# Moving the in-weight forms of the attention part from GpSimd to VectorE

## The chip, the cores and the metric

The kernel runs on one core of a Trainium2 chip. A core has five engines that work side by side, each through its own instructions in order: TensorE (PE: matrix products, its weight loads are shown apart as PEld), VectorE (DVE), ScalarE (ACT), GpSimd (POOL) and SyncE (SP), which here only issues DMAs. The metric is the time of one execution on the device in microseconds (us). The kernel before the change takes 964.0 us, the median of 3 runs (963.87 to 964.06).

## The reference

An attention block with routing, and behind it a two-layer block with a gate. Cut to what matters:

```python
# q, k, v: (4, 8, 768, 64); centroids: (8, 16, 64)
q_assign = argmax(einsum('bhsd,hcd->bhsc', q_n, c_n))     # q_n, k_n, c_n: normed to length 1
k_assign = argmax(einsum('bhsd,hcd->bhsc', k_n, c_n))
mask = q_assign[:, :, :, None] == k_assign[:, :, None, :]
scores = where(mask, q @ k.T / sqrt(64), -1e9)
attn = exp(scores - max(scores)); attn = attn / (sum(attn) + 1e-9)
x = (attn @ v), as (3072, 512)                            # (batch, token) rows, (head, d) columns
h = x @ w_in                                              # w_in: (512, 2048)
g = h * erf(max(h, 0) + log1p(exp(-abs(h))))
out = g @ w_out                                           # w_out: (2048, 512)
```

## The kernel before

**Two parts.** The attention part comes first and takes the first 411 us or so. It goes through 16 *pairs* (a batch and two heads that lie in the two halves of the 128 partitions). The second part computes `x @ w_in` and `g @ w_out` in 2x2 blocks with seven block products in place of eight (in places in two levels, with fewer still). For this it needs sums and differences of blocks of the weights and of `x`. These sums and differences are called *forms*.

**The forms.** `left_forms` (line 632) lists four of them for one slice of `w_in`, `right_forms` (641) four for a slice of `x`. Each is one instruction that reads two tiles of 128 x 512 float32 in SBUF and writes one. Forms of a slice depend on each other: the first feeds the second, the third overwrites a block of `w_in` in place, the fourth needs the second. The kernel makes a list of forms before the attention part starts (1338 to 1340): four slices of `w_in`, so 16 forms, each entry with a version for VectorE (`[0]`) and one for GpSimd (`[1]`). Behind pair 13 four forms of the first chunk of `x` join the list (line 1513). Whoever makes the next form takes the first entry off the list, so the order of the forms is fixed and only the engine and the place differ.

**The periods.** `period(p, i)` (line 1344) writes the instructions of one sixth of a pair. There are two halves of the queries to a pair and six blocks of 128 keys to a half, hence 12 units; a period has two, `u` and `u + 1`, and three periods make a half. A period holds, in this order in each engine's own queue:

- *Maxima of the next pair* (`maxima_step`, 462). For the shift of the softmax the kernel needs row maxima ahead of time. TensorE multiplies low-precision copies into `wide`, a single PSUM buffer, and VectorE reduces it into `nmx` (0.96 us). A period has two such steps. Because `wide` is one buffer, TensorE refills it only after VectorE has reduced it.
- *Scores* (`products`, 513, and `scores`, 526). TensorE writes the products of queries and keys and the masks into `sc`, of which there are two buffers; ACT takes the exponential (`curve`, 540) into one of eight `pr` tiles.
- *Sums* (`accumulate`, 549). POOL adds the `pr` tiles of the period before into an accumulator, ten additions of 128 x 768 to a pair, 1.7 to 1.8 us each.
- *Products with v* (`attend`, 561), on TensorE into `turned`.
- *Division* (`divide`, 574), in periods 0 and 3, for the half that just ended. TensorE multiplies the accumulator with `minus` (the row sums), so it waits for POOL's last addition. ACT makes the inverse, VectorE multiplies (`den`, `turned`, `more_out`), and SP stores the result in four DMAs.
- *Routing of the pair after next* (`similarities`, 393, and `choose`, 406). In period 3 TensorE writes similarities, and VectorE transposes them (`sims`), takes their maxima and marks the winners (`hot`). These maxima lie in the score bank `sc` of the period's second unit, so TensorE can't reuse that bank before `hot` is made. The masks `km` and `qm` come of this in later periods; the one that VectorE makes in period 0 (`km`, 436) serves the prediction as a mark for a pair's start.
- *Weights*. The weights lie in memory as 64-bit numbers and are made into float32 in steps: up to pair 14, each pair converts two pieces, with ACT (`size`, `rest`, `sign`), VectorE (`bounded` and `shifted`, 0.4 us each: both in period 0, and one and one in period 3) and POOL (`summed`, 1.29 us, in periods 1 and 4, which also has SP fetch a further piece).
- *Forms*, as below.

The order within an engine is the order in which the program writes its instructions (`InOrder`, line 129); no planner moves them. Between the engines only semaphores order the work.

**Where the forms stand.** `FORMS` (line 41) says how many forms VectorE makes in which period of which pair: `FORMS[p][i]`. `POOL_FORMS` (line 42) says in which pairs POOL makes one. The lines are

```python
        for _ in range(min(len(forms), FORMS.get(p, {}).get(i, 0))):
            forms.pop(0)[0]()
        ...
            for w in (u - 2, u - 1):
                accumulate(w)
            if i == 4 and p in POOL_FORMS and forms:
                forms.pop(0)[1]()
```

VectorE's forms come after `bounded` and, in period 0, `shifted`; in period 3 they come between `bounded` and `sims`. POOL's come behind its additions of the period, and ahead of the next period's. What is left on the list behind the last pair is made by VectorE (line 1514), ahead of the last additions. Before the change VectorE makes 1 form each in the pairs 12 and 13 (period 0), 2 in pair 14 (periods 0 and 3), 7 in pair 15 and 1 behind the loop; POOL makes one each in the pairs 8 to 15, in period 4.

Of the kernel before, what the change touches and what calls it, by code (L numbers as in the profile page):

```python
# [28 lines left out]
HJ = NJ // 2  # L29
# [8 lines left out]
LC = 512  # L38

UP = 2.0**16  # L40
FORMS = {12: {0: 1}, 13: {0: 1}, 14: {0: 1, 3: 1}, 15: {0: 1, 3: 2, 4: 2, 5: 2}}
POOL_FORMS = range(8, 16)
BIG = 2.0**60
FLOOR = 2.0**50
EPS = 2.0**-70
# [100 lines left out]
def kernel(  # L146
# [174 lines left out]
    def bounded(n):  # L321
        w = w_steps[n][0]
        ve.tensor_scalar(out=w, in0=w, scalar1=2.0, scalar2=None, op0=ALU.max)
# [5 lines left out]
    def shifted(n):  # L329
        w = w_steps[n][0].bitcast(U32)  # L330
        ve.tensor_scalar(out=w, in0=w, scalar1=3, scalar2=None, op0=ALU.logical_shift_left)
# [61 lines left out]
    def similarities(p):  # L393

        if p >= NPAIR:
            return
        st = pairs[p]
        st["psim"] = turned[1][:, 0:HW]
        for g in range(4):
            te.matmul(  # L400
                st["psim"][2 * C * g : 2 * C * (g + 1)], lhsT=ccT[:, p % HP],
                rhs=st["qk"[g // 2] + "T"][:, (g % 2) * HW : (g % 2 + 1) * HW],
                start=True, stop=True,
            )
# [27 lines left out]
    def vectors(p, nm):  # L432
        if p < NPAIR:
            ae.copy(out=pairs[p][nm + "v"], in_=pairs[p][nm + "T"])

    def masks(p, nm, half, bank, narrow=False, copied_by=ae):

        if p >= NPAIR:
            return lambda: None
        st = pairs[p]  # L440
        cols = slice(half * HW, (half + 1) * HW)
        r, hot = slice(0, D) if nm == "q" else slice(D, P), st["hotT"]
        picked = pick[r, half]
        if narrow:
            r = slice(r.start + Q, r.stop)
            picked = pick[r, 1]
            hot = hot if half else st["aside"]
        won = bank[:, 0:HW]
        te.matmul(won, lhsT=picked, rhs=hot[r], start=True, stop=True)
        if nm == "q":  # L450
            return lambda: ae.activation(out=st["qm"][:, cols], in_=won, func=ACT.Relu)
        if copied_by is ve:
            return lambda: ve.tensor_scalar(
                out=st["km"][:, cols], in0=won, scalar1=BIG, scalar2=nbig, op0=ALU.mult, op1=ALU.add
            )
        return lambda: ae.activation(
            out=st["km"][:, cols], in_=won, func=ACT.Identity, bias=nbig, scale=BIG
        )
# [34 lines left out]
    def turn(p, h, copies=(ae.copy, ae.copy)):  # L493

        st = pairs[p]
        pn = turned[h][:, 0:HW].rearrange("p (t n) -> p t n", t=HJ)
        for t in range(HJ):
            for e in range(2):
                cols = slice(e * D, e * D + Q)
                te.matmul(pn[cols, t], lhsT=lowest[h][:, t, cols], rhs=identb, start=True, stop=True)  # L500
        for e, copy in zip(range(2), copies):
            r = slice(e * D, e * D + 1)
            copy(out=st["qm"][r, h * HW : (h + 1) * HW], in_=pn[r].rearrange("p t n -> p (t n)"))
        st["shift", h] = True
# [8 lines left out]
    def products(u):  # L513
        p, half, j = units[u]
        if u in sc_of:
            return
        st = pairs[p]
        sc = sc_of[u] = ps_s.tile([P, 2, 512], F32, name="sc", tag="s")
        for e in range(2):
            r = slice(e * D, (e + 1) * D)  # L520
            te.matmul(
                sc[:, e, 0:HW], lhsT=st["kT"][r, j * P : (j + 1) * P],
                rhs=st["qT"][r, half * HW : (half + 1) * HW], start=True, stop=False,
            )

    def scores(u, rows=Q):

        p, half, j = units[u]
        st = pairs[p]
        sc = sc_of[u]  # L530
        assert ("shift", half) in st
        for e in range(2):
            r = slice(e * D, (e + 1) * D)
            r = slice(r.start, r.start + rows)
            te.matmul(
                sc[:, e, 0:HW], lhsT=st["km"][r, j * P : (j + 1) * P],
                rhs=st["qm"][r, half * HW : (half + 1) * HW], start=False, stop=True,
            )

    def curve(u):  # L540

        pr = prs[u % NPT]
        sc = sc_of.pop(u)[:, :, 0:HW].rearrange("p e (c x) -> p e c x", c=2)
        ae.activation(out=pr[:, :, :, 0:QW], in_=sc, func=ACT.Exp, scale=D**-0.5)
# [780 lines left out]
    def run(work):  # L1325
        for _ in work:
            pass
# [3 lines left out]
    def step_ahead(u, behind=False):  # L1331
        p, i = divmod(u + NJ, 2 * NJ)
        steps = maxima_step(p, i, behind=behind) if p < NPAIR else iter(())
        if not behind:
            run(steps)
        return steps

    forms = []
# [5 lines left out]
    def period(p, i):  # L1344
        u = 2 * NJ * p + 2 * i
        n1, n2 = 2 * p - 1, 2 * p
        early = lambda n: 0 <= n < N_EARLY

        def mask(place):
            which = (MASKS if p else FIRST_MASKS).get((i, place))  # L1350
            if which:
                return masks(p + 1, *which, turned[0 if i in (0, 5) else 1], place > 1, ve if i == 0 else ae)
            return lambda: None

        if u > 0:
            for which in turns if i in (0, 3) else ():
                turn(*which)
                turns.remove(which)
            step_ahead(u)
        mask(0)()  # L1360
        next(part[0], None)
        if i == 5:
            next(routing[0], None)
        if i == 0 and p:
            run(routing[0])
        if u == 2:
            next(routing[0])
        products(u)
        products(u + 1)
        mask(1)()  # L1370
        second = step_ahead(u + 1, True) if u > 0 else iter(())
        next(second, None)
        rows = D if u == 0 or u + NJ >= len(units) else Q
        scores(u, rows)
        next(second, None)
        if i:
            next(second, None)
        next(part[0], None)
        scores(u + 1, rows)
        later = mask(2)  # L1380
        if i == 0:
            later()
            later = lambda: None
            next(second, None)
        if i == 3:
            similarities(p + 2)
            routing[0] = choose(p + 2, sc_of[u + 1][:, 0], True)
        curve(u)
        later()
        curve(u + 1)  # L1390
        if u == 0:
            step_ahead(1)
            similarities(1)
            routing[0] = choose(1, turned[0])
            next(routing[0])
            next(routing[0])
            vectors(1, "q")
            vectors(1, "k")
        if i == 0 and early(n1 - 1):
            bounded(n1 - 1)  # L1400
            shifted(n1 - 1)
            sign(n1 - 1)
        elif i == 1 and early(n1):
            size_and_rest(n1)
        elif i == 3 and early(n1):
            bounded(n1)
            sign(n1)
        elif i == 5 and early(n2):
            rest(n2)
        for _ in range(min(len(forms), FORMS.get(p, {}).get(i, 0))):  # L1410
            forms.pop(0)[0]()
        if i == 3:
            next(routing[0], None)
            if early(n1):
                shifted(n1)
            for _ in range(2):
                next(routing[0], None)
        elif i == 1:
            load(p + 1, "v", v, vp)
            if p == 0:  # L1420
                run(routing[0])
                transposes(2, "q")
        elif i == 2:
            transposes(p + 2, "k")
        elif i == 4:
            vectors(p + 2, "k")
            vectors(p + 2, "q")
        elif i == 5:
            transposes(p + 3, "q")
        if u > 0:  # L1430
            if i == 1 and early(n1 - 1):
                summed(n1 - 1)
            elif i == 4 and early(n1):
                summed(n1)
            for w in (u - 2, u - 1):
                accumulate(w)
            if i == 4 and p in POOL_FORMS and forms:
                forms.pop(0)[1]()
            for w in (u - 2, u - 1):
                attend(w)  # L1440
            if i % HJ == 0:
                part[0] = divide(u - 1)
                next(part[0])
        if i == 3 and early(n2):
            size(n2)
# [204 lines left out]
```

## Time and profile before

| | |
|---|---|
| time, median of 3 runs | 964.0 us |
| the profiled execution | 963.7 us |
| its span in the trace | 962.0 us |
| pairs 7 and 8, from `km` to `km` | 24.44, 24.43 us |
| pairs 9 to 13 | 24.97, 24.81, 24.79, 25.03, 25.04 us |
| end of the attention part on TensorE | 411.5 us |
| VectorE's form of 128 x 512 | 0.68 to 0.69 us in pairs 12 to 14; 0.80 to 2.18 us in pair 15 |
| POOL's form of 128 x 512 | 1.27 to 1.29 us |
| TensorE clock granted | 1.00 in the windows of the attention part |

The trace is read as follows. The page gives busy times of the engines and the chain of work that ended last. The order in time gives each instruction's start and duration, its engine and operation, the tiles it writes and reads (`nmx<-wide`), shapes, the number merged into one line, and in brackets how long the engine was idle before it and what ended that wait. Most lines of the kernel are recorded under one line, L137, the helper that passes instructions on; so instructions are told apart by their tiles. A form is a `TENSOR_TENSOR` of 128x512 whose tiles are `w_in`, `more_in`, `x_own` or `x_more`. The tile `more_out` is used for several things in the attention part, POOL's accumulators among them. A window gives the busy time of each engine between two moments.

### The profile page before, as it was taken

How to read it: one execution, taken by the hardware profiler on the slowest of the kernel's cores; microseconds unless marked ns; L12 is line 12 of the kernel's file. 1: busy time of each engine (PE TensorE's matmuls, PEld its weight loads, DVE VectorE, ACT ScalarE, POOL GpSimd, SP SyncE). 2: the span in 40 equal slices, each digit the busy share in tenths (PEclk: the TensorE clock that was granted, in tenths of full speed). 3: DMA queues.
4: the chain of work that ended last, by engine and by line, in shares of the span. 5: the costliest groups of instructions: out<-in, count | busy, mean ns of one | idle time of the engine just before them, and what ended most of it. 6: DMA issues, size and time to landing. Idle time of an engine off the chain costs nothing.

```text
span 962.0 us, 22444 instructions
## 1 busy us (share of the span) xinstructions
PE 951.8 (99%) x8954; PEld 727.4 (76%) x8954; DVE 798.2 (83%) x1399; ACT 538.9 (56%) x815; POOL 531.4 (55%) x371
## 2 busy tenths in 40 slices
PE   8999999999999999999999999999999999999998
PEld 3555555555555555588888888998999899989987
DVE  8888888888888887787579889788868987897887
ACT  3777777777777777552523541654257236625541
POOL 1688888888888888887479910360054016202600
PEclk9999999999999999999999999999999999999999
DMA  9354444454453521051404444363445336343433
GB/s 220 65 111 112 111 111 111 112 112 110 106 111 76 126 57 54 23 174 44 165 1 163 164 136 141 133 204 112 155 123 174 112 129 209 110 147 119 159 114 110
DMA packets 172313, 116.06 MB, mean 121 GB/s; under 512 B 131376, under 2 KB 141104, under 8 KB 172208
## 3 DMA queue, kind: packets, MB, share of 16 engines
q1 hardware_dynamic: 169280, 113.41, 42.1%
q8 instruction: 71, 1.16, 0.5%
q10 hardware_dynamic: 2928, 1.21, 0.4%
q14 instruction: 34, 0.28, 0.1%
HBM read 90.21 MB, written 24.38 MB: 119 GB/s over the span
## 4 chain that ended last, share of the span: by engine, by line
PE 96%; DVE 2%; DMA 1%; POOL 0%; issue 0%; ACT 0%; SPq 0%; DVEq 0%; POOLq 0%
PE bank L137 42%; PE turned L137 31%; PE sc L137 17%; PE wide L137 6%; DVE nmx L137 1%; DVE km L137 0%; POOL more_out L137 0%; DMA in_k<-in_k_dram 0%; SPq L137 0%; DMA in_q<-in_q_dram 0%; DVE kT L137 0%; ACT qm L137 0%; DVE sims L137 0%; DVE qT L137 0%; ACT pr L137 0%
## 5 line engine op out<-in xcount | busy, mean ns | idle before, releaser
L137 POOL TENSOR_TENSOR more_out<-more_out,pr 128x768 f32<-128x768 f32 x128 | 217.1, 1696 | 15.7 <-ACT pr L137 6.8
L137 DVE TENSOR_REDUCE nmx<-wide 128x2 f32<-128x768 f32 x189 | 180.5, 955 | 47.1 <-PE wide L137 46.5
L137 ACT ACTIVATE pr<-sc 128x768 f32<-128x768 f32 x192 | 148.8, 810 | 89.7 <-PE wide L137 76.0
L137 POOL TENSOR_TENSOR g<-g 128x512 f32<-128x512 f32 x36 | 47.1, 1309 | 217.2 <-DVE g L137 215.3
L137 PE MATMUL turned<-pr,in_v 128*32 128x193 f32 x3072 | 144.9, 330 | 0.0
L137 PEld LDWEIGHTS turned<-pr,in_v 128*32 128x32 f32 x3072 | 91.5, 109 | 50.7 <-issue 21.3
L137 PE MATMUL sc<-qT,kT 64*128 64x384 f32 x528 | 98.4, 486 | 0.0
L137 DVE TENSOR_TENSOR g<-g 128x512 f32<-128x512 f32 x114 | 79.1, 694 | 16.5 <-PE bank L137 12.9
L137 DVE TENSOR_TENSOR g<-bank,g 128x256 f32<-128x256 f32 (+1 forms) x129 | 63.9, 523 | 16.2 <-PE bank L137 9.1
L137 DVE TENSOR_TENSOR g<-a_s,g 128x512 f32<-128x512 f32 x80 | 72.4, 932 | 5.6 <-ACT a_s L137 5.6
L137 PE MATMUL bank<-w_out,g 128*128 128x256 f32 x328 | 75.7, 380 | 0.0
L137 ACT ACTIVATE a_s<-g 128x1024 f32<-128x1024 f32 (+1 forms) x36 | 41.0, 1149 | 56.3 <-POOL g L137 45.7
L137 PE MATMUL bank<-g_more,g 128*128 128x256 f32 x304 | 71.8, 379 | 0.0
L137 PE MATMUL bank<-x_own,w_in 128*128 128x128 f32 (+1 forms) x432 | 71.6, 308 | 0.0
L137 POOL TENSOR_TENSOR more_out<-pr,pr 128x768 f32<-128x768 f32 x32 | 59.3, 1853 | 19.9 <-ACT pr L137 19.9
L137 PEld LDWEIGHTS bank<-w_out,g 128*128 128x128 f32 x328 | 62.0, 190 | 9.6 <-issue 1.4
L137 PEld LDWEIGHTS <-qv 64*128 64x128 bf16 x384 | 26.9, 93 | 53.4 <-issue 37.3
L137 PEld LDWEIGHTS sc<-qT,kT 64*128 64x128 f32 x528 | 50.1, 187 | 21.3 <-ACT inv L137 3.1
L137 PE MATMUL wide<-kv,qv 64*128 64x384 bf16 x378 | 64.3, 328 | 1.2 <-ACT km L137 0.6
L137 ACT ACT_TABLE_LOAD x40 | 51.3, 1283 | 23.0 <-DVE g L137 22.4
L137 PEld LDWEIGHTS bank<-x_own,w_in 128*128 128x128 f32 x432 | 61.1, 191 | 4.0 <-issue 0.6
L137 PEld LDWEIGHTS bank<-g_more,g 128*128 128x128 f32 x304 | 57.8, 190 | 7.9
(244 smaller groups left out, 2059.5 us busy)
## 6 DMA issues: line engine op xcount, KB each, us to landing
g_more<-b_dram SPq DMA_DIRECT2D x48, 512.0 KB, 3.5
g_more<-w_dram SPq DMA_DIRECT2D x84, 256.0 KB, 2.8
x_own<-in_moe_w_in_dram SPq DMA_DIRECT2D x13, 512.0 KB, 5.1
in_v<-in_v_dram SPq DMA_DIRECT2D x32, 192.0 KB, 3.1
x_dram<-more_out SPq DMA_DIRECT2D x128, 48.0 KB, 1.7
x_own<-x_dram SPq DMA_DIRECT2D x6, 1024.0 KB, 5.7
in_k<-in_k_dram SPq DMA_DIRECT2D x59, 96.0 KB, 2.7
in_q<-in_q_dram SPq DMA_DIRECT2D x58, 96.0 KB, 4.8
```

What stands on the lines that cost most here:

```text
L137: ins = getattr(self.engine, name)(*args, **kw)
```

## The change

`FORMS` has VectorE make two forms in each of the pairs 8 to 15, one in period 0 and one in period 3. `POOL_FORMS` has only pair 15, where POOL makes two, in the periods 1 and 4 (`HJ` is 3). What is left behind the last pair is still made by VectorE.

```diff
-FORMS = {12: {0: 1}, 13: {0: 1}, 14: {0: 1, 3: 1}, 15: {0: 1, 3: 2, 4: 2, 5: 2}}
-POOL_FORMS = range(8, 16)
+FORMS = {p: {0: 1, 3: 1} for p in range(8, 16)}
+POOL_FORMS = (15,)
...
-            if i == 4 and p in POOL_FORMS and forms:
+            if i % HJ == 1 and p in POOL_FORMS and forms:
                 forms.pop(0)[1]()
```

In numbers: of the 20 forms, VectorE made 12 and POOL 8; now VectorE makes 18 and POOL 2. Two, in place of one, are left for VectorE behind the loop. By the end of pair 13, twelve forms are made in place of eight; the forms of `x` are the last four either way.

## The prediction

> **What bounds the kernel now.** I read the profile's page first (busy shares, chain), then windows that cut the span at the pairs of the attention part, then the order in time of VectorE and TensorE around the two places where the change puts work.
>
> ```profile
> PE 951.8 (99%) x8954; PEld 727.4 (76%) x8954; DVE 798.2 (83%) x1399; ACT 538.9 (56%) x815; POOL 531.4 (55%) x371
> ...
> PE 96%; DVE 2%; DMA 1%; POOL 0%; issue 0%; ACT 0%; SPq 0%; DVEq 0%; POOLq 0%
> ```
>
> TensorE carries 96% of the chain. So only an edit that makes TensorE wait, or removes such a wait, moves the time. Next the windows, one for each of the pairs 7 to 13 (pair 11's, 290.56 to 315.35, is left out: 24.79), cut where VectorE writes `km` in period 0 (start:end, length, then busy PE, PEld, DVE, ACT, POOL):
>
> ```profile
> 191.91:216.35 24.44, 24.44 (x360) 13.88 (x356) 21.02 (x35) 19.18 (x32) 19.63 (x13) 1.00 0.50 110
> 216.35:240.78 24.43, 24.43 (x360) 13.90 (x356) 21.01 (x34) 19.16 (x32) 19.69 (x14) 1.00 0.49 109
> 240.78:265.75 24.97, 24.78 (x360) 14.03 (x356) 20.90 (x35) 19.15 (x32) 20.81 (x14) 1.00 0.49 107
> 265.75:290.56 24.81, 24.61 (x360) 14.03 (x356) 21.01 (x34) 19.18 (x32) 20.82 (x14) 1.00 0.50 108
> ...
> 315.35:340.38 25.03, 24.78 (x360) 14.02 (x355) 21.51 (x35) 19.17 (x32) 20.90 (x14) 1.00 0.50 108
> 340.38:365.42 25.04, 24.80 (x360) 14.03 (x356) 20.55 (x34) 19.17 (x32) 20.90 (x14) 1.00 0.21 55
> ```
>
> Pairs 7 and 8 take 24.43 with TensorE never idle. Pairs 9 to 11, each behind a POOL form, take 24.97, 24.81, 24.79; pairs 12 and 13, which also have a VectorE form in period 0, take 25.03 and 25.04. What a form costs in each place can be read from this. Period 0, in pair 8 (no form ahead of it) and then in pair 12 (a POOL form behind it and a VectorE form in it), from the order in time:
>
> ```profile
> 217.47 0.51 PE L137 MATMUL turned<-more_out,minus 128*32 128x192 f32 x8
> ...
> 218.54 0.95 DVE L137 TENSOR_REDUCE nmx<-wide 128x2 f32<-128x768 f32 x1
> ...
> 219.54 0.34 PE L137 MATMUL wide<-kv,qv 64*128 64x384 bf16 x2
> ...
> 316.86 0.53 PE L137 MATMUL turned<-more_out,minus 128*32 128x192 f32 x8 [0.21 <-POOL more_out L137]
> ...
> 317.54 0.69 DVE L137 TENSOR_TENSOR more_in<-w_in 128x512 f32<-128x512 f32 x1
> 318.14 0.95 DVE L137 TENSOR_REDUCE nmx<-wide 128x2 f32<-128x768 f32 x1
> ...
> 319.15 0.34 PE L137 MATMUL wide<-kv,qv 64*128 64x384 bf16 x2
> ```
>
> `wide` is one buffer: TensorE can refill it only when VectorE's reduction of it is over. In pair 8 the reduction ends at 219.49 and the refill starts at 219.54, so VectorE has no slack there even without a form. Measured from `km`, the refill is at 3.19 in pair 8 (from 216.35) and at 3.80 in pair 12 (from 315.35): 0.61 later. And period 3 with the start of period 4, in pair 8:
>
> ```profile
> 228.98 0.42 DVE L137 TENSOR_SCALAR w_in<-w_in 128x512 f32<-128x512 f32 x1
> ...
> 229.32 0.58 DVE L137 STREAM_TRANSPOSE sims<-turned 128x384 f32<-128x384 f32 x1
> ...
> 230.71 0.55 DVE L137 TENSOR_TENSOR hot<-sims,sc 128x384 bf16<-128x384 f32 x1
> ...
> 231.18 0.95 DVE L137 TENSOR_REDUCE nmx<-wide 128x2 f32<-128x768 f32 x1
> ...
> 231.38 0.33 PEld L137 LDWEIGHTS sc<-more_out 64*128 64x128 f32 x4 [0.34 <-ACT inv L137]
> ...
> 232.18 0.34 PE L137 MATMUL wide<-kv,qv 64*128 64x384 bf16 x2
> ```
>
> VectorE runs without a gap from 228.11. Two things of TensorE wait for it: the second products' weights (the score bank holds the maxima that `hot` reads; `hot` ends at 231.26, the load goes at 231.38; that the profile names ACT there is an inference, ACT's `inv` was done) and the refill of `wide` (reduction over at 232.13, refill at 232.18). No slack here either.
>
> **The change part by part.**
>
> *A form on VectorE in period 0 of pairs 8 to 11* (pairs 12 to 14 have it already). One instruction, 0.69 alone; the next starts 0.60 after it (317.54 to 318.14). Price on the path 0.61, from pair 12. Bounds: a form put in front of others on an in-order engine makes none earlier, so not under 0; at most 2.12, what a VectorE form took at 399.50 beside a busy POOL.
>
> *A form on VectorE in period 3 of pairs 8 to 13* (pair 14 has it already). It goes between `bounded` and `sims`. Behind it on VectorE: `sims`, `shifted`, the maxima, `hot`, the reduction; waiting for those: TensorE as shown. No pair before has routing and a form in period 3 together, so I bound it: 0 if 0.6 of slack were hidden that the order in time doesn't show; 2.12 with POOL in the way. I take 0.60, the step of the row in pair 14 (378.99 to 379.60), since slack is 0.05 and POOL is idle there (its sums end at 229.10, its next instruction comes at 230.98).
>
> *POOL's form in period 4 of pairs 8 to 14 goes.* It is 1.28 ahead of four sums of 6.97 that end at 242.22 in pair 9, and TensorE's row sums (`minus`) start at 242.27, 1.49 after `km`, against 1.12 in pair 8. That is worth 0.37 in pairs 9 to 11. In pairs 12 and 13 it is worth nothing: the form's 0.61 in period 0 is counted from `km`, and covers it. After the change the sums end about 0.9 ahead of need, the wait is gone, and late next is the reduction.
>
> So pairs 8 to 13 each take 24.43 + 0.61 + 0.60 = 25.64, or 153.84. Before they took 365.42 - 216.35 = 149.07. That is +4.77. (Pair 9's last 0.17 went with a transpose of `in_k` that waited 0.35; I take it as not coming again.)
>
> *Pairs 14 and 15.* Pair 14 keeps its two VectorE forms. Its lost POOL form matters at the start of pair 15:
>
> ```profile
> 390.43 1.97 DVE L137 TENSOR_TENSOR more_in<-w_in,more_in 128x512 f32<-128x512 f32 x1
> ...
> 391.90 0.53 PE L137 MATMUL turned<-more_out,minus 128*32 128x192 f32 x8 [0.85 <-POOL more_out L137]
> ```
>
> In pair 8 the row sums start 1.34 after the products that precede them (216.13 to 217.47); here that is 389.53 + 1.34 = 390.87. POOL, 1.28 earlier, would end at 390.57. So 391.90 - 390.87 = 1.03 comes back. Bounds 0 and 1.03.
>
> In pair 15 VectorE's forms fall from 7 to 2, with 2 more behind the loop in place of 1; POOL makes 2 in place of 1, the new one in period 1, where POOL was idle for 1.57 before 395.63. I cost all of it at nothing: from 391.90 to the end of attention TensorE has no idle time. If that cover is gone, POOL's sums, which end at 403.16 just ahead of row sums at 403.22, are late by up to 1.28. The last x form ended at 415.56 before and its product came at 416.79; with two forms fewer in line it is ready sooner. Behind attention TensorE isn't idle from 411.5 to 900, and nothing there changes.
>
> No DMA is issued by a form. SP's stores of the attention output follow VectorE's division and shift with it; POOL's `summed`, which issues a fetch on SP, starts from ACT's sign step, 1.7 after the new form would begin, so no queue is passed.
>
> Sum: +4.77 - 1.03 = +3.74 on the profiled 963.7, which stands 0.3 under the median: 964.0 + 3.74 = **967.7**.
>
> One rule of the Trainium skill speaks for the change and one against. Its page "GPSIMD Engine Reference", section 4.1 Engine selection, sends elementwise work to VectorE, about twice as fast for two inputs; the trace agrees (0.69 against 1.28), and by engine time alone six forms moved would save 3.5. But the same page, section 8 Key points, says that the two engines share SBUF interfaces and contend where VectorE has two SBUF inputs. The trace shows 1.97 to 2.18 for such forms beside POOL's sums in pair 15; were all ten new forms of pairs 8 to 13 so, the sum would be 14 higher (rival 3).
>
> **The rivals.**
>
> 1. *Period 3 has slack* (a no-change case). Then only period 0 pays: 6 x 25.04 - 149.07 = +1.17, less 1.03: 964.1. For it: a wait is ascribed to ACT there. Against: two separate edges of 0.05 to 0.12 behind VectorE.
>
> 2. *POOL was the price, VectorE's forms are free* (faster). The one mechanism is TensorE's wait for POOL's sums at each period 0: 0.54, 0.38, 0.36, then 0.37 twice, and 1.03: -3.05, or 960.9. It decides if VectorE has 0.6 to spare in both periods; pairs 12 and 13 cost 0.24 more than 10 and 11, against it.
>
> 3. *Forms collide with POOL*: 2.06 in place of 0.69, or 1.37 for each. In period 3 alone, 6 x 1.37 = 8.2: 975.9. For it: pair 15. Against: POOL's idle gaps of 1.2 and 1.9 at both places, and pairs 12 to 14 with 0.69 in them.
>
> 4. *POOL's form in period 1 of pair 15, or the order there, gives the 1.03 back*: 968.7.
>
> **How the numbers follow.** Forecast 0.72 (966.5 to 968.3 by the small bounds: 0.17 for pair 9, 0.09 x 10 for a form that costs its 0.69), rival 4 0.10, rival 1 0.08 with partial slack in period 3 besides, rival 3 0.07, rival 2 0.03. The range leaves out rivals 1 to 3, 0.18 together, and reaches toward them: 965.2 (period 3 at 0.2 each) to 969.8 (rival 4 with 0.69 a form). A measurement tells 0.2%, or 1.9, from no change. Faster is rival 2, 0.03; within 0.2% is rival 1 and period 3 under 0.3 each, 0.12; slower the rest, 0.85.
>
> **What would show it.** Right: pairs 8 to 13 at 25.6 each, no TensorE wait for POOL in period 0, a TensorE gap of about 0.6 before `wide` in periods 0 and 4, forms at 0.69, row sums of pair 15 without a wait. Wrong: pairs near 25.0 (slack), forms near 2 (collision), or a wait for POOL in pair 15's period 3. What would break the sum is a second buffer's worth of slack that I don't see, or POOL's sums moving, once their form is gone, onto VectorE's new forms.

## The result, and the profile after

The changed kernel takes **967.64 us** (median of 6 runs, 967.34 to 967.72) where the kernel before, timed beside it, takes 964.03 (963.87 to 964.22): a ratio of 1.0037, with a 95% interval of 1.0024 to 1.0050. It is slower by 3.6 us. The forecast was 967.7. The profiled execution took 967.34 us, with a span of 965.6 in place of 962.0.

The windows of the changed kernel, cut where VectorE writes `km`, then at the row sums of pair 15, at the end of the attention part on TensorE and at the end (start:end, length, then busy PE, PEld, DVE, ACT, POOL):

```profile
191.92:216.36 24.44, 24.44 (x360) 13.88 (x356) 21.01 (x35) 19.16 (x32) 19.63 (x13) 1.00 0.51 110
216.36:241.99 25.63, 24.79 (x360) 14.13 (x356) 22.11 (x36) 19.41 (x32) 19.77 (x13) 1.00 0.45 104
241.99:267.62 25.63, 24.79 (x360) 14.12 (x356) 22.11 (x36) 19.38 (x32) 19.68 (x13) 1.00 0.48 105
...
344.52:370.16 25.64, 24.80 (x360) 14.14 (x356) 21.15 (x36) 19.38 (x32) 19.71 (x13) 1.00 0.20 54
370.16:395.60 25.44, 24.99 (x376) 14.82 (x372) 19.12 (x31) 17.67 (x29) 19.92 (x13) 1.00 0.14 33
...
415.18:965.50 550.32, 546.73 (x3292) 499.62 (x3288) 447.29 (x822) 238.80 (x330) 209.38 (x157) 1.00 0.42 135
```

Pair 7 is as before. Each of the pairs 8 to 13 takes 25.63 or 25.64, so pair 14 begins at 370.16 and not at 365.42: 4.74 later. From there to the row sums of pair 15 it is 25.44, against 26.48 before (365.42 to 391.90): 1.04 come back. What follows the attention part takes 550.3 as before (411.5 to 961.9 was 550.4). 4.74 - 1.04 = 3.70 in the trace, beside 3.61 in the times.

The waits of TensorE in the changed kernel (who waited, for whom, in total, how often, the longest):

```profile
PE wide L137 <- DVE nmx L137: 3.6, 9, 0.5
...
PE turned L137 <- DVE sims L137: 2.3, 6, 0.4
```

Both are new at this size: before, TensorE waited 0.4 for `nmx` and 2.0 for POOL's sums (`more_out`), and that last wait is gone. Pair 8 of the changed kernel in order of time, first its period 0, then its period 3:

```profile
218.55 0.69 DVE L137 TENSOR_TENSOR more_in<-w_in 128x512 f32<-128x512 f32 x1
...
219.15 0.95 DVE L137 TENSOR_REDUCE nmx<-wide 128x2 f32<-128x768 f32 x1
...
220.16 0.34 PE L137 MATMUL wide<-kv,qv 64*128 64x384 bf16 x2 [0.46 <-DVE nmx L137]
...
229.93 0.68 DVE L137 TENSOR_TENSOR more_in<-more_in,w_in 128x512 f32<-128x512 f32 x1
...
230.53 0.57 DVE L137 STREAM_TRANSPOSE sims<-turned 128x384 f32<-128x384 f32 x1
...
231.25 0.53 PE L137 MATMUL turned<-more_out,minus 128*32 128x192 f32 x8 [0.39 <-DVE sims L137]
...
232.39 0.95 DVE L137 TENSOR_REDUCE nmx<-wide 128x2 f32<-128x768 f32 x1
...
233.39 0.34 PE L137 MATMUL wide<-kv,qv 64*128 64x384 bf16 x2
```

In period 0 the refill of `wide` comes 3.80 after `km` (216.36), where it came 3.19 after it in pair 8 before: 0.61. In period 3 the form pushes `sims` by 0.60 (229.32 before, shifted by period 0's 0.61 to 229.93, now 230.53). TensorE's row sums wait for `sims`, because the kernel writes the similarities and these row sums to the same columns of PSUM, in `turned[1]` (`similarities` and `divide`). There was no slack in this before the change either: `sims` ended at 229.90, and the row sums came right behind it, as they do now (231.10 and 231.25):

```profile
230.07 0.51 PE L137 MATMUL turned<-more_out,minus 128*32 128x192 f32 x8
```

The refill of `wide` comes at 233.39, 0.05 behind the end of the reduction; before it was 232.18, so both prices, 1.21, have arrived by then. Not all of this is booked as a wait: TensorE is idle for 0.46 before the refill in period 0 and for 0.39 before the row sums, and its busy time in the pair is 24.79 in place of 24.43. The forms of pair 8 take 0.68 to 0.69.

### The profile page after: what moved, and what is told of

It reads as the page before. It is cut to its first block, busy times and chain, and to the rows that moved or that the text cites. A ratio compares the mean times of both kernels' runs of the same rounds, so it can differ in the third digit from the quotient of the medians.

```text
span 965.6 us, 22445 instructions
## 1 busy us (share of the span) xinstructions
PE 952.2 (99%) x8954; PEld 728.3 (75%) x8954; DVE 795.4 (82%) x1405; ACT 540.2 (56%) x815; POOL 522.4 (54%) x365
## 3 DMA queue, kind: packets, MB, share of 16 engines
q10 hardware_dynamic: 2928, 1.21, 0.4%
## 4 chain that ended last, share of the span: by engine, by line
PE 93%; DVE 5%; DMA 1%; issue 1%; SPq 0%; DVEq 0%; ACT 0%
PE bank L137 42%; PE turned L137 29%; PE sc L137 16%; PE wide L137 6%; DVE nmx L137 3%; DVE more_in L137 1%; DVE w_out L137 0%; DVE km L137 0%; DVE sims L137 0%; DMA in_k<-in_k_dram 0%; DVE w_in L137 0%; SPq L137 0%; DMA in_q<-in_q_dram 0%; DVE kT L137 0%; DVE qT L137 0%
## 5 line engine op out<-in xcount | busy, mean ns | idle before, releaser
L137 ACT ACTIVATE a_s<-g 128x1024 f32<-128x1024 f32 (+1 forms) x36 | 41.0, 1149 | 55.6 <-POOL g L137 44.9
```

The lines of the kernel that those rows point to most:

```text
L137: ins = getattr(self.engine, name)(*args, **kw)
```

## The experiments

### Each form's price, alone and together

The expectations call it an edge where TensorE can go on only when another engine has done its part. Three kernels leave forms of VectorE out, a fourth leaves out GpSimd's. The first, from the changed kernel (the memsets are the same in all four):

```diff
         for _ in range(min(len(forms), FORMS.get(p, {}).get(i, 0))):
-            forms.pop(0)[0]()
+            work = forms.pop(0)[0]
+            if not (8 <= p < 14 and i == 3):
+                work()
...
+        if p == 0 and i in (1, 2, 4):
+            ge.memset(more_in[:, i // 2], 0.0)
```

> The changed kernel with VectorE's forms in period 3 of pairs 8 to 13 left out (six forms are not made; three memsets on GpSimd in pair 0 stand in for their tiles, so the values of these blocks are not the reference's). Edge theory (every 0.60 that VectorE adds in period 3 is a TensorE wait): 6 x 0.60 goes, 964.0 us, pairs 8 to 13 at 25.03 to 25.04. Rival, one shared budget of VectorE a pair (the second form pays only because the first has used the slack up): the form that stays still pays, but less than 0.6, so pairs under 24.9 and a time under 963.2. Rival, the period-3 form is nearly free: 966 or more.

Measured: 964.39 us, a ratio of 1.0004 (0.9995 to 1.0014) to the kernel before. The second has `i == 0` in the condition, the third no condition on the period:

> The changed kernel with VectorE's forms in period 0 of pairs 8 to 13 left out instead (same stand-ins). Edge theory: 6 x 0.61 goes, 964.0 us, pairs 8 to 13 at 25.03, with TensorE's wait for the transposed similarities and for the reduction still there in periods 3 and 4. Shared-budget rival: pairs under 24.9. Period-3-free rival: pairs at 24.43, about 960.4.

Measured: 964.52 us, ratio 1.0005 (0.9996 to 1.0014).

> The changed kernel with all twelve forms of pairs 8 to 13 left out (same stand-ins). Edge theory: both prices go and they add, 12 x 0.605 = 7.26 less, 960.4 us, pairs at 24.43 as pairs 3 to 8 were before. If something else of the change costs (queues, instruction stream), pairs stay above 24.43.

Measured: 960.65 us, ratio 0.9965 (0.9951 to 0.9979). The windows of pair 8, of the kernel with period 0's forms only, of the one with period 3's only, and of the one with none:

```profile
216.77:241.80 25.03, 24.58 (x360) 14.12 (x356) 21.52 (x35) 19.15 (x32) 19.73 (x13) 1.00 0.47 106
```

```profile
216.46:241.49 25.03, 24.64 (x360) 13.87 (x356) 21.61 (x35) 19.39 (x32) 19.66 (x13) 1.00 0.47 106
```

```profile
216.42:240.86 24.44, 24.44 (x360) 13.88 (x356) 21.02 (x35) 19.18 (x32) 19.64 (x13) 1.00 0.49 109
```

24.44 with none, 25.03 with either, 25.63 with both: each form costs 0.59 to 0.60, whether or not the other is there. That is what the edge theory says, and the shared budget is out. The times are 0.2 to 0.5 above the expected ones. Part of this is that single pairs stand out by 0.1 to 0.2 (pair 12 of the first kernel, 25.22; pair 9 of the second, 25.20; pairs 9 and 12 of the third, 24.61 and 24.56). Another part is at the start: pair 8's mark is at 216.42 to 216.77 in place of 216.36. The memsets needn't be the cause of that, since kernels without them, further down, have the mark at up to 216.74 too.

> The kernel before with GpSimd's forms of pairs 8 to 14 left out (seven forms not made; same stand-ins), VectorE's as before. Edge theory: GpSimd's form pays 0.37 only where VectorE has no form in the next period 0: pairs 10 and 11 go to 24.43, pair 9 too or to 24.6 if its late transpose stays, pairs 12 and 13 stay at 25.03; pair 15's wait gives 1.03 back: 961.7 us (961.9). Rival, GpSimd's price adds to VectorE's: pairs 12 and 13 fall to 24.66 too, 960.9.

The edit, on the kernel before:

```diff
             if i == 4 and p in POOL_FORMS and forms:
-                forms.pop(0)[1]()
+                work = forms.pop(0)[1]
+                if p == 15:
+                    work()
```

Measured: 961.96 us, ratio 0.9977 (0.9967 to 0.9987). Pairs 9, 10 and 12 of it:

```profile
241.19:265.79 24.60, 24.60 (x360) 13.88 (x356) 20.91 (x35) 19.17 (x32) 19.61 (x13) 1.00 0.51 109
265.79:290.23 24.44, 24.44 (x360) 13.87 (x356) 21.01 (x34) 19.15 (x32) 19.64 (x13) 1.00 0.49 110
314.67:339.70 25.03, 24.58 (x360) 14.13 (x356) 21.52 (x35) 19.18 (x32) 19.73 (x13) 1.00 0.48 108
```

Pair 10 drops from 24.81 to 24.44, pair 12 stays at 25.03. GpSimd's form thus paid only where no VectorE form stood in the period 0 behind it. Pair 9 keeps 0.17: its transpose of `in_k` waits 0.34 with no form near, so the forms are not the cause; what it waits for was not followed. In the changed kernel this wait doesn't come. That is not because its pairs are longer: pair 12 of the kernel with period 0's forms only and pair 9 of the one with period 3's only, both with pairs of 25.03, have it (0.36 and 0.35).

### One part alone: the last pairs

```diff
-POOL_FORMS = range(8, 16)
+POOL_AT = [(p, 4) for p in range(8, 14)] + [(15, 1), (15, 4)]
...
-            if i == 4 and p in POOL_FORMS and forms:
+            if (p, i) in POOL_AT and forms:
```

> The kernel before with one part of the change alone: GpSimd makes no form in pair 14 and makes one more in period 1 of pair 15 instead; all other places as before, so the last pair's forms on VectorE each come one later in the list or stay. The prediction's term: pair 15's row sums don't wait, 1.03 less, 963.0 us, and the form in period 1 of pair 15 costs nothing. Rival, the wait comes back in pair 15 (its sums in period 3 end 0.06 ahead of the row sums): 964.0.

Measured: 963.02 us, ratio 0.9990 (0.9981 to 0.9999). The row sums of pair 15 in this kernel, without a wait:

```profile
390.85 0.51 PE L137 MATMUL turned<-more_out,minus 128*32 128x192 f32 x8
```

They came at 391.90 before. This part of the change gains 1.03 by itself, and GpSimd's form in period 1 of pair 15 costs nothing.

### What of period 3 is the price

```diff
-        for _ in range(min(len(forms), FORMS.get(p, {}).get(i, 0))):
-            forms.pop(0)[0]()
+        if i != 3:
+            for _ in range(min(len(forms), FORMS.get(p, {}).get(i, 0))):
+                forms.pop(0)[0]()
         if i == 3:
             next(routing[0], None)
             if early(n1):
                 shifted(n1)
             for _ in range(2):
                 next(routing[0], None)
+            for _ in range(min(len(forms), FORMS.get(p, {}).get(i, 0))):
+                forms.pop(0)[0]()
```

> The changed kernel with VectorE's form of period 3 moved behind the marking of the winners, so that the similarities are transposed and the score bank is given back as early as without a form; only the reduction of the next period is behind it. TensorE's six waits for the transposed similarities (2.3 us together in the changed kernel's waits) go. Theory, VectorE's last edge decides: the 0.60 comes back whole at the refill of the maxima's buffer, 967.6 us, pairs 8 to 13 at 25.63. Rival, the wait for the similarities is the price of period 3: 6 x 0.38 goes, 965.3, pairs at 25.25.

Measured: 973.63 us, ratio 1.0100 (1.0085 to 1.0115): slower than either theory said, pairs at 26.59. Pair 8 of this kernel in order of time:

```profile
231.06 0.51 PE L137 MATMUL turned<-more_out,minus 128*32 128x192 f32 x8
...
231.97 1.29 POOL L137 TENSOR_TENSOR w_in<-w_in,x_own 128x512 int32<-128x512 int32 x1 [2.37 <-ACT x_own L137]
...
232.17 1.64 DVE L137 TENSOR_TENSOR more_in<-more_in,w_in 128x512 f32<-128x512 f32 x1
...
233.73 0.95 DVE L137 TENSOR_REDUCE nmx<-wide 128x2 f32<-128x768 f32 x1
...
234.73 0.34 PE L137 MATMUL wide<-kv,qv 64*128 64x384 bf16 x2 [1.42 <-DVE nmx L137]
```

The wait for the similarities is gone (the row sums don't wait), and period 3 costs more than before, 1.56 a pair (26.59 against the 25.03 of period 0's forms alone). That is just the time by which the form holds up the reduction (232.17 to 233.73). So the last edge, the reduction, passes a delay on in full by itself, and the wait for `sims` in the changed kernel was only the first place where the delay shows. The excess over 0.60 is a collision: the form starts 0.2 behind GpSimd's sum of the weights (231.97 to 233.26), ends 0.55 after it, and takes 1.64 where 0.69 is its own time. GpSimd's next sum takes 2.26 in place of 1.83.

The page "GPSIMD Engine Reference" of the Trainium skill, section 8 Key points, says that GpSimd contends with VectorE instructions that have two SBUF inputs or run in a two-port mode. The 1.64 agrees with it.

### VectorE's idle places

```diff
-        for _ in range(min(len(forms), FORMS.get(p, {}).get(i, 0))):
+        for _ in range(min(len(forms), FORMS.get(p, {}).get(i, 0) if p > 14 else 0)):
...
             step_ahead(u)
+        if 8 <= p < 15 and i in (2, 3):
+            forms.pop(0)[0]()
         mask(0)()
```

> The changed kernel with the two VectorE forms of pairs 8 to 14 moved to where VectorE was idle for 0.96 and 0.83: between the two reductions of period 2 and of period 3. GpSimd is in its additions there. Idle-time theory: 0.60 fits into each gap, pairs 8 to 13 at 24.43 and pair 14 0.6 shorter: 967.6 - 7.2 - 0.6 = 959.8 us. Contention theory (a VectorE form waits for GpSimd's running addition and holds the next up): forms at 1.3 to 2.1 each; what they take over 0.9 or so and what GpSimd's additions then lack before the row sums comes back on TensorE, up to 0.7 a form: 961 to 967, pairs at 24.6 to 25.4.

Measured: 964.37 us, ratio 1.0004 (0.9994 to 1.0013); pairs at 25.11, inside what contention allowed. In pair 8:

```profile
223.49 1.27 DVE L137 TENSOR_TENSOR more_in<-w_in 128x512 f32<-128x512 f32 x1
...
227.60 1.02 DVE L137 TENSOR_TENSOR more_in<-more_in,w_in 128x512 f32<-128x512 f32 x1
...
229.41 1.06 DVE L137 TENSOR_SCALAR w_in<-w_in 128x512 f32<-128x512 f32 x1
...
231.10 0.53 PE L137 MATMUL turned<-more_out,minus 128*32 128x192 f32 x8 [0.45 <-DVE sims L137]
```

Both forms fit their gaps in spite of 0.3 to 0.6 of waiting for GpSimd. But they held GpSimd's additions up twice, so the last addition now ran into `bounded`, which took 1.06 in place of 0.42. That is 0.64 of the 0.67 a pair: a collision passed on to a stretch of VectorE with no slack.

### GpSimd's idle places

GpSimd's form moved from period 4 to period 3, where GpSimd was idle, on the kernel before:

```diff
-            if i == 4 and p in POOL_FORMS and forms:
+            if i == 3 and p in POOL_FORMS and forms:
                 forms.pop(0)[1]()
```

> The kernel before with GpSimd's form moved from period 4 to period 3, where GpSimd was idle for 1.9 to 2.4 us ahead of the weights' sum; VectorE's forms as before, no form on VectorE in pairs 8 to 11. Theory: GpSimd's additions end in time for period 0, so pairs 10 and 11 lose their 0.37 and pair 15 its 1.03; but the weights' shift on VectorE (two-port form) now meets a running GpSimd form and waits up to 0.6 for it, at the edge of period 3: pairs 8 to 11 at 24.4 to 25.0, 961.9 to 965.5 us. Without contention 961.9.

Measured: 966.67 us, ratio 1.0028 (1.0018 to 1.0038), above the range; pairs 8, 10 and 11 at 25.06 to 25.07, and pairs 9, 12 and 13 at 25.66 to 25.75. From pair 8, VectorE first, then GpSimd:

```profile
230.21 1.02 DVE L137 TENSOR_SCALAR w_in<-w_in 128x512 uint32<-128x512 uint32 x1
```

```profile
229.47 1.47 POOL L137 TENSOR_TENSOR more_in<-w_in 128x512 f32<-128x512 f32 x1
```

`shifted` takes 0.64 more than its 0.38 and ends 0.29 behind the form's end (230.94): it waits for the form, as expected. In pair 9, where GpSimd's form starts just ahead of `bounded` (254.51 and 254.60), `bounded` waits instead and takes 1.48. I had seen the first collision and not the second.

With `shifted` moved behind `hot` besides:

```diff
         if i == 3:
-            next(routing[0], None)
+            for _ in range(3):
+                next(routing[0], None)
             if early(n1):
                 shifted(n1)
-            for _ in range(2):
-                next(routing[0], None)
```

> The same, with the weights' shift of period 3 moved on VectorE behind the marking of the winners, out of the GpSimd form's way. Theory: no engine that TensorE waits for has more to do at either edge: pairs 8 to 11 at 24.43, pairs 12 and 13 at 25.03 for their VectorE form in period 0, 1.03 back in pair 15: 961.9 us, which would beat both kernels. If the order of the routing steps costs (the maxima right behind the transpose), up to 0.2 a pair over all pairs, 964.

Measured: 967.89 us, ratio 1.0041 (1.0026 to 1.0056): missed. The pairs from 1 on, those without a form too, take 24.66 to 24.68 in place of 24.44, apart from 9, 12 and 13, in which GpSimd's form still collides with `bounded` (25.90 to 25.98). The order in time of pair 8 shows one place: the maxima start 0.68 behind the start of `sims` when they come next on VectorE, and `shifted` starts 0.49 behind it when it stands between. So `shifted` had in part been filling a wait of the maxima, which read `sims`; from `sims` to the reduction it is now 2.09 in place of 1.86.

### A version that is faster than both

The first try has one VectorE form a pair, in period 2's gap of pairs 7 to 14, and no GpSimd form before pair 15. Against the kernel before:

```diff
-FORMS = {12: {0: 1}, 13: {0: 1}, 14: {0: 1, 3: 1}, 15: {0: 1, 3: 2, 4: 2, 5: 2}}
-POOL_FORMS = range(8, 16)
+FORMS = {14: {3: 1}, 15: {0: 1, 3: 2, 4: 2, 5: 2}}
+POOL_AT = [(15, 1), (15, 4)]
...
+        if 7 <= p < 15 and i == 2:
+            forms.pop(0)[0]()
         mask(0)()
...
-            if i == 4 and p in POOL_FORMS and forms:
+            if (p, i) in POOL_AT and forms:
...
-            forms += zip(*(right_forms(e, *x_parts(0)) for e in (ve, ge)))
+            forms[:0] = zip(*(right_forms(e, *x_parts(0)) for e in (ve, ge)))
```

> A version built from the runs so far: one VectorE form a pair, in pairs 7 to 14, between the two reductions of period 2 (where VectorE was idle for 0.96); no GpSimd form before pair 15, which has two; VectorE's form in period 3 of pair 14 and seven in pair 15 as before; the four forms of x taken ahead of the last forms of the weights. Edge theory with the collision seen in the period-2 place (a form of 1.27, hidden): pairs 7 to 13 at 24.43 to 24.5, pair 14 0.6 shorter than before, pair 15's wait of 1.03 gone: 964.0 - 2.5 - 0.6 - 1.0 = 959.9 us (960.4 if a late transpose of k comes twice or thrice). If the last forms of the weights, behind the loop, hold up the eviction of the first products, up to 1 back: 961.

Measured: 964.09 us, ratio 1.0001 (0.9992 to 1.0010): missed. Pairs 7 to 13 take 24.73 to 24.77, 0.32 over 24.44, and the second part lost 2 us. In pair 7, and at the end of attention:

```profile
229.31 0.72 DVE L137 TENSOR_SCALAR w_in<-w_in 128x512 f32<-128x512 f32 x1
...
415.83 1.13 PE L137 MATMUL bank<-x_more,w_in 128*128 128x256 f32 x4 [0.66 <-ACT g L137]
```

`bounded` again meets GpSimd's additions, late by one collision. And the first eviction of the second part (the copy of a finished product out of PSUM) waits for GpSimd's last addition. That ends at 415.38, about where it ended before (415.01), though TensorE begins the second part 1.78 earlier; GpSimd had waited 1.76 for a VectorE form that its own form needs. Of the 2 us, 0.9 are lost by the next row sums (7.16 after the part's start, before 6.24); the rest was not followed. The second try, shown against the first, transposes the similarities ahead of `bounded`, and makes the last four forms of the weights among the first products of the second part:

```diff
-FORMS = {14: {3: 1}, 15: {0: 1, 3: 2, 4: 2, 5: 2}}
-POOL_AT = [(15, 1), (15, 4)]
+FORMS = {14: {3: 1}, 15: {0: 1, 3: 2, 4: 2}}
+POOL_AT = [(15, 1)]
...
-        if 7 <= p < 15 and i == 2:
+        if 7 <= p and i == 2:
             forms.pop(0)[0]()
...
-            bounded(n1)
             sign(n1)
...
             next(routing[0], None)
             if early(n1):
+                bounded(n1)
                 shifted(n1)
...
-    for work, _ in forms:
-        work()
...
-    aside_work += idle(3) + all_weights(0, 4) + out_forms[0] + out_forms[1]
+    aside_work += [work for work, _ in forms] + all_weights(0, 4) + out_forms[0] + out_forms[1]
```

> The version of period 2 again with its two losses taken away. In period 3 the similarities are transposed ahead of the weights' bound, so the bound, which waits for GpSimd's last addition, no longer holds TensorE's row sums. At the end of the attention part GpSimd makes one form only (period 1 of pair 15), VectorE makes none behind period 4 of pair 15, and the last four forms of the weights are made among the first products of the second part. Edge theory: pairs 7 to 13 at 24.43 (they were 24.76), the attention part ends near 407.3, no wait of TensorE for the first eviction: 964.0 - 2.5 - 0.6 - 1.0 = 959.9 us. Rival: the bound's wait only moves on to the reduction at the end of the same stretch (pairs 24.7, 962), or the four late forms hold up evictions (up to 1 each).

Measured: 964.46 us, ratio 1.0003 (0.9994 to 1.0012): missed. Pairs take 24.67 to 24.70 from pair 1 on (pair 6, 24.83), those without a form as well: the changed order costs 0.24 everywhere. A form in the gap of pair 15 also took 2.09 and made TensorE wait 0.82 for `lowest`. The third keeps the order in period 3 and moves `bounded` forward into the gap between period 3's reductions, for the pairs with a form in period 2; from the first try:

```diff
-        if 7 <= p < 15 and i == 2:
+        if 7 <= p < 15 and i == 2 or p == 14 and i == 3:
             forms.pop(0)[0]()
+        if 7 <= p < 14 and i == 3:
+            bounded(n1)
...
         elif i == 3 and early(n1):
-            bounded(n1)
+            if not 7 <= p < 14:
+                bounded(n1)
```

> One VectorE form a pair between the two reductions of period 2 in pairs 7 to 14, and in pairs 7 to 13 the weights' bound (0.42) is moved forward to between the two reductions of period 3 (VectorE was idle for 0.83 there), so that it neither meets GpSimd's last addition ahead of the similarities nor makes them late; pair 14 has two more forms, in the gap of period 3 and at its end; no GpSimd form before pair 15, and the last pair's forms as in the kernel before, with the four forms of x taken first. Edge theory: the bound's wait for GpSimd ends inside the gap, pairs 7 to 13 at 24.43 to 24.5; pair 14 0.4 to 0.6 shorter than before, pair 15's wait of 1.03 gone; the tail as before: 959.8 to 960.5 us. If GpSimd's additions, delayed twice, end behind the row sums' time in period 3, up to 0.4 a pair comes back: 963. If the edge theory is wrong in that VectorE's load as such counts (its total work in these pairs is as in the period-2 version), pairs stay at 24.76 and the time at 962 to 964.

Measured: **960.42 us** (960.32 to 960.60), ratio 0.9962 (0.9949 to 0.9976) to the kernel before: 3.6 us faster than before and 7.2 faster than the change. Pairs 7 to 11 take 24.39 to 24.40, a little less than without forms (24.44), for a reason that stays open; pair 12, in which the transpose of `in_k` waits 0.35, takes 24.67, and pair 13 24.37. Pairs 8 to 13 together take 146.6 where they took 149.07 before, and from the start of pair 14 to the end of the attention part it is 44.9 in place of 46.1. Pairs 7 and 8, roughly (the windows begin 0.4 ahead of their marks), and `bounded` in pair 7:

```profile
191.89:216.34 24.45, 24.45 (x359) 13.93 (x352) 22.52 (x35) 19.16 (x31) 20.01 (x13) 1.00 0.48 110
216.34:240.80 24.46, 24.46 (x359) 13.93 (x352) 22.54 (x35) 19.16 (x31) 20.12 (x13) 1.00 0.47 109
```

```profile
227.56 0.75 DVE L137 TENSOR_SCALAR w_in<-w_in 128x512 f32<-128x512 f32 x1
```

VectorE is busier here than in the changed kernel, 22.5 in 24.45 against 22.1 in 25.63, and TensorE isn't idle in these windows at all. `bounded` still waits for GpSimd, inside the gap. The kernel before without GpSimd's forms of pairs 8 to 14, which saves seven forms, gained only 2.1: this one makes all 20.

## Why the prediction was right

- *The form in period 0*: forecast 0.61, from the refill of `wide` in pairs 8 and 12. Measured 0.59 alone (25.03 against 24.44), 0.60 on top of the other (25.63 against 25.03) and 0.61 in the order in time.
- *The form in period 3*: forecast 0.60 with nothing in the trace of before that had it. Measured 0.59 alone and 0.60 on top of the other. The size was right; the step's mechanism was incomplete. The prediction named two things that wait for VectorE there, the second products' weights and the refill. A third waits first: the row sums, 0.39 on `sims`. The form behind `hot` took this wait away and made nothing faster, since the last edge by itself passes the whole delay on. So one of the prediction's signs came only in part: a TensorE gap of about 0.6 before `wide` in periods 0 and 4 was forecast, and there are 0.46 in period 0, none in period 4 and 0.39 before the row sums.
- *Pairs 8 to 13 together*: forecast 25.64 each and +4.77, measured 25.63 to 25.64 and +4.74. That the 0.17 of pair 9 doesn't come again held too, by luck: no reason was given for it, and other kernels have the same wait again in one pair.
- *GpSimd's form gone*: forecast 0.37 in pairs 9 to 11, nothing in 12 and 13. The kernel without these forms showed both. In the changed kernel GpSimd's sums end at 242.27 and the row sums come at 243.11: 0.84 of slack, where some 0.9 was forecast.
- *Pair 15*: forecast -1.03, measured -1.04, and -1.03 alone. The rest of pair 15 and the second part at nothing: both held.
- *Rivals.* Slack in period 3 (964.1): out by the kernel with period 3's forms alone. VectorE's forms free (960.9): out by the same kernels. Collisions (975.9): not in the changed kernel's pairs 8 to 14, where the forms took 0.68 to 0.69 (in its pair 15 one took 2.12, as before, and TensorE did not wait for it); but all seven experiments that move a form or `shifted` within the pairs 7 to 14 have collisions there. The 1.03 given back (968.7): out.
- *The range.* Its inner bounds don't follow from the terms beside them: 0.17 and 0.09 x 10 on top of 967.7 are 968.8, not 968.3, and nothing there gives 966.5. And the upper bound for a form, 2.12, is under the 2.18 that the same text reads in pair 15. The measured 967.64 depends on neither.

## What to carry to other kernels

Ask of an instruction that is put on a busy engine what stands behind it and who waits for that, at that very place: here VectorE had 3.4 us to spare in a pair of 24.4 (21.0 busy), and still 0.6 cost 0.6 in two places, and nothing in the gap of period 2 once `bounded` was out of the way too. An engine's idle time is worth something only where the next thing that others wait for lies behind the gap and not ahead of it. And look at what runs at that moment on GpSimd: a place that is free in the order of one engine can be taken on the other (forms took 1.0 to 1.6 there in place of 0.69).

## What was not expected of the hardware

Collisions of VectorE and GpSimd are very regular in these traces. A form (128 x 512 float32, two SBUF inputs, on VectorE) that starts beside a running GpSimd instruction ends 0.55 after that instruction's end. This holds, to 0.01, in all 113 cases of the runs in which a form took 0.77 to 2.18 beside one (from 180 to 413 us). GpSimd's next instruction is longer by 0.3 to 0.4 (2.26 in place of 1.83 in the kernel with the form behind `hot`, 2.02 in place of 1.68 in the kernel with forms in VectorE's idle places). One-input operations of VectorE on float32 and on integers in SBUF wait as well and end 0.28 to 0.29 after the GpSimd instruction, in 32 cases (`bounded` 0.42 to 1.06 and 1.48, `shifted` 0.38 to 1.02). Reductions and transposes of PSUM beside GpSimd keep their times (0.95 and 0.57). Why the ends lie at these distances was not tried apart; the runs show only the durations.
